# One PSUM pool of four banks for products and values, two banks lent as a third score slot, three scheduling rules, and longer assumed DMA latencies

## The chip, the cores and the metric

The kernel runs on one core of one Trainium2 chip. The metric is the device time of one execution in microseconds, the median of several runs. All runs in this document are of the state that the measurements call fast. Each kernel was timed in alternation with the kernel before on the same chip. A ratio below is the mean time of one kernel's fast runs over the mean time of the other's fast runs of the same rounds, so it is not quite the ratio of the medians that are quoted.

## The reference

Two blocks, each run twice in turn, on 2048 tokens of width 640, in bf16:

```python
x = A_x
x = x + _A_ref(_layernorm(x), ...)   # attention: 32 heads of 20, 4 segments of 512 tokens
x = x + _B_ref(_layernorm(x), ...)   # feed-forward: 640 -> 1728 -> relu -> 640
x = x + _A_ref(_layernorm(x), ...)
x = x + _B_ref(_layernorm(x), ...)
# inside _A_ref, for each segment s of 4:
    p = softmax(qs @ ks.T * scale + causal mask); a_dot = p @ vs
    a_mem = phi(qs) @ M / (phi(qs) @ z + 1e-6)           # memory of the earlier segments
    o = g * a_mem + (1 - g) * a_dot
    M += phi(ks).T @ vs;  z += sum(phi(ks))
```

## The kernel before: the parts that matter here

The kernel is written as about thirty generators ("streams"), one for each kind of work. A list scheduler inside the Python program takes the next operation of some stream again and again, with assumed durations, and writes out one fixed instruction list for each engine. At run time there is no choice any more. If an engine's next instruction has to wait, what stands behind it in the list is held up too: in one run below (a_latold) TensorE stood still for 2.18 us in front of one product. The assumed numbers therefore shape the order, and nothing else.

```python
X = Slot(ps[:, 0:2, :], "SX")                    # two score slots of two PSUM banks
Y = Slot(ps[:, 2:4, :], "SY")
OD = Slot(ps[:, 4, :], "OD")                     # one bank for p @ v ("values")
MISC = [Slot(ps[:, 5 + k, :], "misc%d" % k) for k in range(3)]   # three for all other products
...
def turn(slot_sem, dst, src, waits):             # a transpose by DMA
    ... yield dma("sp", ..., e.dma_start_transpose(dst, src), waits,
            issue=max(1400.0, 140.0 * n), lat=2000.0, rate=270.0, holds=True)
...
# scores(): a round is two halves (two heads each), half k goes to (X, Y)[k]
both = pe(221.0, fns, a[1] + b[1] + a[0].tks + b[0].tks, take=[a[0], b[0]], mode="rows")
...  # while no layer norm of block B has begun, one half alone is allowed too ("lone")
# exps(): ACT reads a whole slot (128x1024) and frees it
tx = yield act(1024, lambda e: e.activation(dst, src, ACT.Exp, scale=SCALE), sc + pw)
bkp.release(tx)
...
# apply(): p @ v of four heads
yield Acq([OD])
tk = yield pe(540.0, fns, mk + vt + OD.tks, mode="cols", lag=COLS_LAG)
...
yield from values_done(a, s, g, tk)              # at a segment's end: wait for "dm", then free v
```

Scores and values use a quarter of the array for each matmul, four at a time. So do 160 small ones of the feed-forward (128*32 in the trace). All other matmuls use the whole array. I call the q, k and v projections of segments 1 and 2 of the first attention *early products*: they need no attention result, so TensorE can do them while segment 0's attention goes on. *Filler* is any product that TensorE can do while attention waits for something. Of the tiles named below, o_sb holds the attention output and oT its transpose, xnT a transposed layer norm, and om_sb the part read from the memory. A *spill* is a transfer to DRAM.

The softmax here doesn't subtract the row's maximum and nothing guards it: scores larger than these inputs give would overflow.

## Time and profile before

| | kernel before |
|---|---|
| time | 582.72 us median of 4 runs (582.07 to 584.15) |
| profiled span | 580.5 us |
| TensorE busy | 562.3 us, 97% |
| ACT, VectorE busy | 413.4 us, 400.8 us |

Lines of the page of the kernel before: the span, the busy time of each engine with its share and instruction count, then busy tenths in 40 equal slices and the granted TensorE clock. In all views PE is TensorE and PEld its weight loads, ACT is ScalarE, DVE is VectorE, POOL is GpSimd; L1048 is line 1048 of that kernel.

```profile
span 580.5 us, 13203 instructions
...
PE 562.3 (97%) x5442; PEld 307.0 (53%) x5442; DVE 400.8 (69%) x1048; ACT 413.4 (71%) x528; POOL 185.7 (32%) x291
...
PE   7999989899999999999999999999999999999998
...
PEclk9999998999999999999999999999999999999999
```

TensorE is the bottleneck, but its busy time hides much. The Trainium skill says so ("Perfetto Trace Analysis", Identifying the Most-Contended Engine: matmul busy time is a bad metric for how close a kernel is to roofline, because matmuls are pipelined), and this trace agrees: a 128x320 matmul is recorded at 299 ns, and the next one starts 136 ns after it. I therefore worked from start times. A whole-array matmul of N columns lets the next one start N/2.4 + 2.6 ns later (136 ns for 320 and 216 ns for 512 columns, as the trace has them; the 21-column ones start 25 ns apart), and about 96 ns more when the tiling of the array changes. Time between two starts beyond that, where it is over 20 ns, I call **lost**. Lost time inside a record of the trace that gives the clock as 0.5 counts as lost to the clock, as far as half rate explains it; the rest counts as lost to waits. Every "lost" below is worked out in this way from one profile.

In the kernel before, 23.2 us are lost: 5.1 in 0 to 40 us, 2.7 in 40 to 80, 6.5 in 80 to 120, and 8.9 later. The stretches of the kernel before, with the busy time of each engine, the granted clock, the DMA share and GB/s:

```profile
core 0: us, PE busy (x) PEld busy (x) DVE busy (x) ACT busy (x) POOL busy (x), PEclk, DMA share, GB/s
30.00:62.00 32.00, 30.71 (x403) 17.36 (x406) 27.84 (x72) 28.18 (x37) 13.23 (x20) 1.00 0.81 192
62.00:80.00 18.00, 17.45 (x202) 9.07 (x195) 17.10 (x50) 16.18 (x22) 7.46 (x12) 1.00 0.79 186
80.00:120.00 40.00, 36.11 (x496) 20.11 (x495) 34.67 (x103) 34.80 (x43) 15.28 (x23) 0.96 0.76 175
120.00:200.00 80.00, 79.05 (x837) 41.27 (x835) 60.83 (x157) 64.36 (x76) 31.45 (x49) 1.00 0.37 86
200.00:320.00 120.00, 118.10 (x1128) 59.90 (x1127) 95.05 (x227) 100.25 (x121) 47.62 (x73) 1.00 0.54 109
320.00:480.00 160.00, 156.58 (x1460) 81.81 (x1458) 115.65 (x315) 119.48 (x152) 52.84 (x80) 1.00 0.39 82
```

From 80 to 120 us TensorE is even recorded as idle for 3.9 us, and the clock is 0.96. What it waits for there (engine and line, who ended the wait; us in total, times, longest):

```profile
PEld ps L1048 <- ACT PT L1100: 4.1, 8, 1.2
PEld ps L941 <- DVE om_sb L952: 2.8, 4, 1.1
...
PE ps L941 <- DVE om_sb L952: 1.4, 3, 0.8
```

L1048 is the scores: they wait for ACT's exps to free both slots. L941 is the reads of the memory. The 0.96 is one record of 3.4 us at clock 0.5, from 88.3 us on. The timeline shows it in the 128x320 matmuls, 0.47 us each where 0.30 is usual:

```profile
87.90 0.86 PE L590 MATMUL ps<-wo_r,oT 128*128 128x320 bf16 x4
88.56 0.47 PE L587 MATMUL ps<-wo_r,oT 128*128 128x320 bf16 x1
88.82 0.47 PE L590 MATMUL ps<-wo_r,oT 128*128 128x320 bf16 x1
```

The last view is ACT's timeline in the middle of segment 0. Two exps take 1.94 us, and then ACT does other work or waits for scores:

```profile
45.38 1.92 ACT L1100 ACTIVATE PT<-ps 128x1024 bf16<-128x1024 f32 x2
48.29 1.94 ACT L1100 ACTIVATE PT<-ps 128x1024 bf16<-128x1024 f32 x2 [0.98 <-PE ps L1048]
50.12 0.60 ACT L764 ACTIVATE w_r<-ps 128x512 bf16<-128x512 f32 x1
51.14 1.94 ACT L1100 ACTIVATE PT<-ps 128x1024 bf16<-128x1024 f32 x2 [0.42 <-PE ps L1048]
```

### The profile page before, as it was taken

The numbers are of one execution on the slowest core, as the hardware profiler recorded it, in microseconds if no ns is written. First come the engines' busy times: TensorE is split into PE (matmuls) and PEld (weight loads), VectorE is DVE, ScalarE is ACT, GpSimd is POOL, SyncE is SP. The second block draws the span as 40 slices with busy tenths as digits, with TensorE's granted clock in tenths as the row PEclk, the third lists the DMA queues.
The fourth block names the chain that finished last, engine by engine and source line by source line (L and its number), as shares of the span: only waits on it lengthen the run. The fifth ranks groups of instructions, "written<-read, shape, count | busy, mean of one in ns | idle before, by whom it ended". The sixth has DMA issues, their size and how long they took to land.

```text
span 580.5 us, 13203 instructions
## 1 busy us (share of the span) xinstructions
PE 562.3 (97%) x5442; PEld 307.0 (53%) x5442; DVE 400.8 (69%) x1048; ACT 413.4 (71%) x528; POOL 185.7 (32%) x291
## 2 busy tenths in 40 slices
PE   7999989899999999999999999999999999999998
PEld 6754545455544443555436545555454554665655
DVE  4879998956988778878678982789836784353202
ACT  5688998878788878887998786877767778214140
POOL 4234343433434334344333441144412443100000
PEclk9999998999999999999999999999999999999999
DMA  8578886633162622964278031781317611433101
GB/s 261 136 159 188 211 210 161 154 116 71 32 172 58 111 41 82 194 98 66 57 190 147 2 66 35 171 166 20 65 38 178 117 42 19 87 69 33 59 1 46
DMA packets 125741, 59.90 MB, mean 103 GB/s; under 512 B 104562, under 2 KB 115570, under 8 KB 125682
## 3 DMA queue, kind: packets, MB, share of 16 engines
q1 hardware_dynamic: 125552, 58.90, 45.9%
q8 instruction: 43, 0.70, 0.5%
q10 hardware_dynamic: 130, 0.16, 0.1%
q14 instruction: 16, 0.13, 0.1%
HBM read 20.57 MB, written 12.85 MB: 58 GB/s over the span
## 4 chain that ended last, share of the span: by engine, by line
PE 77%; DVE 14%; DMA 5%; ACT 2%; issue 0%; SPq 0%; POOL 0%
PE ps L590 50%; PE ps L587 11%; PE ps L1048 7%; PE ps L1133 4%; DVE stats L598 2%; DMA otk<-otu 2%; PE ps L1172 2%; ACT PT L1100 1%; PE ps L992 1%; PE ps L941 1%; DVE x_sb L1253 1%; DVE xn_tok L640 1%; DVE stg L763 1%; DVE o_sb L1225 1%; DVE otu L1143 1%; PE ps L1304 1%
## 5 line engine op out<-in xcount | busy, mean ns | idle before, releaser
L1100 ACT ACTIVATE PT<-ps 128x1024 bf16<-128x1024 f32 x320 | 310.0, 1022 | 74.5 <-PE ps L1048 74.1
L1112 POOL TENSOR_SCALAR_AFFINE_SELECT PT<-PT 128x512 bf16<-128x512 bf16 x256 | 164.3, 659 | 293.6 <-ACT PT L1100 293.6
L590 PE MATMUL ps<-w_r,hT 128*128 128x320 bf16 x768 | 124.5, 299 | 0.0
L590 PE MATMUL ps<-xnT,w_r 128*128 128x512 bf16 x416 | 114.1, 379 | 0.0
L1253 DVE TENSOR_TENSOR x_sb<-x_sb,ps 128x320 bf16<-128x320 bf16 x128 | 60.7, 481 | 69.2 <-PE ps L590 68.6
L590 PEld LDWEIGHTS ps<-w_r,hT 128*128 128x128 bf16 x768 | 72.9, 98 | 32.1 <-issue 5.4
L1048 PE MATMUL ps<-pad 20*128 20x512 bf16 (+3 forms) x1024 | 64.4, 302 | 2.4 <-ACT PT L1100 2.4
L590 PEld LDWEIGHTS ps<-xnT,w_r 128*128 128x128 bf16 x416 | 39.3, 98 | 43.4 <-issue 4.2
L598 DVE BATCH_NORM_STATS2 stats<-x_sb 128x6 f32<-128x320 bf16 x124 | 55.1, 474 | 3.6 <-DMA x_sb<-in_A_x_dram 3.0
L1331 ACT ACTIVATE hT<-ps 128x512 bf16<-128x512 f32 x60 | 36.0, 599 | 23.2 <-PE ps L590 23.0
L590 PE MATMUL ps<-wo_r,oT 128*128 128x320 bf16 x256 | 47.6, 305 | 0.0
L1048 PEld LDWEIGHTS ps<-pad 20*128 20x128 bf16 x1024 | 18.7, 92 | 51.7 <-ACT PT L1100 27.2
L587 PE MATMUL ps<-xnT,w_r 128*128 128x512 bf16 x104 | 39.6, 381 | 0.5 <-DVE M_sb L1004 0.5
L1329 DVE TENSOR_SCALAR hT<-ps 128x512 bf16<-128x512 f32 x44 | 30.1, 684 | 12.8 <-PE ps L590 12.5
L1143 DVE CAST otu<-ps 128x512 bf16<-128x512 f32 x43 | 29.4, 683 | 12.8 <-PE ps L1133 12.2
L590 PE MATMUL ps<-wv_r,xnT 128*128 128x320 bf16 x192 | 36.6, 300 | 0.0
L1133 PE MATMUL ps<-PT,v_aug 128*21 128x512 bf16 (+3 forms) x768 | 34.7, 301 | 0.0
L590 PE MATMUL ps<-xnT,wq_r 128*128 128x512 bf16 (+1 forms) x140 | 33.7, 349 | 0.0
L590 PE MATMUL ps<-xnT,wk_r 128*128 128x512 bf16 (+1 forms) x140 | 33.6, 349 | 0.0
L909 ACT ACTIVATE stg<-stg 128x512 bf16<-128x512 bf16 x50 | 31.1, 635 | 2.5 <-DVE rtmp L907 2.5
L612 POOL TENSOR_TENSOR rstd<-lnU,mhalf 128x4 f32<-128x4 f32 (+1 forms) x17 | 16.9, 997 | 45.4 <-DVE lnU L608 40.2
L590 PEld LDWEIGHTS ps<-wo_r,oT 128*128 128x128 bf16 x256 | 24.1, 99 | 12.0 <-issue 3.4
(114 smaller groups left out, 699.1 us busy)
## 6 DMA issues: line engine op xcount, KB each, us to landing
pad<-scr SPq DMA_DIRECT2D x124, 80.0 KB
scr<-stg SPq DMA_DIRECT2D x34, 256.0 KB, 3.0
out_dram<-x_sb SPq DMA_DIRECT2D x16, 160.0 KB, 1.8
w_r<-in_B_w_dram SPq DMA_DIRECT2D x10, 216.0 KB, 3.6
w_r<-in_B_w_dram SPq DMA_DIRECT2D x13, 160.0 KB, 2.8
x_sb<-in_A_x_dram SPq DMA_DIRECT2D x10, 160.0 KB, 3.3
scr<-w_r SPq DMA_DIRECT2D x5, 256.0 KB, 3.3
x_sb<-in_A_x_dram SPq DMA_DIRECT2D x3, 320.0 KB, 7.4
```

What stands on the lines that cost most here:

```text
L587: bk, tk = yield pe(mm_ns(n), [(lambda e, bk, a=a, b=b: e.matmul(bk.ap[:, 0:n] if len(b.shape) == 2 else bk.ap[:, 0:n].rearrange("p (i n) ...
L590: tk = yield pe(mm_ns(n), [(lambda e, k=k, a=a, b=b, bk=bk: e.matmul(bk.ap[:, 0:n] if len(b.shape) == 2 else bk.ap[:, 0:n].rearrange("p (i ...
L598: tk = yield dve(320, 1, lambda e, c2=c2: e.bn_stats(stats6[:, t % 12, c2, :], x_sb[:, t, c2 * 320:(c2 + 1) * 320]), xt)
L909: te = yield act(512, lambda e, q=q: e.activation(q, q, ACT.Exp), [tr] + p, psum=False)
L1048: fns.append([(lambda e, z=z, j=j, hh=hh, N=N, o=o, sl=sl: e.matmul(ps[:, hh, o:o + N], sl.ap[32 * hh:32 * hh + DH, z, 0, 128 * j:128 * j ...
L1100: tx = yield act(1024, lambda e, dst=dst, src=src: e.activation(dst, src, ACT.Exp, scale=SCALE), sc + pw)
L1112: tm = yield pool(600.0, lambda e, reg=reg: e.affine_select(out=reg, in_=reg, pattern=[[0, 4], [1, 128]], compare_op=ALU.is_ge, fill=0.0, ...
L1133: fns.append((lambda e, j=j, hh=hh: e.matmul(OD.ap[32 * hh:32 * hh + DH + 1, 128 * j:L], VAUG[vx(a, s)][:, j, 4 * g + hh, :], pt.ap[:, hh, ...
L1143: te = yield evac(L, 1, lambda e: e.tensor_copy(dst, OD.ap), lambda e: e.activation(dst, OD.ap, ACT.Copy), [tk] + OTU[0].tks)
L1253: ta = yield dve(320, 1, lambda e: e.tensor_tensor(x_sb[:, t, 320 * hf:320 * hf + 320], x_sb[:, t, 320 * hf:320 * hf + 320], bk.ap[:, 0:32 ...
L1329: th = yield evac(512, 1, lambda e, dc=dc, bk=bk: e.tensor_scalar(hT[:, dc, :], bk.ap[:, :], 0.0, None, ALU.max), lambda e, dc=dc, bk=bk: ...
L1331: lambda e, dc=dc, bk=bk: e.activation(hT[:, dc, :], bk.ap[:, :], ACT.Relu), [tk] + HT.tks)
```

## The change

The intent: products and values share four banks. While segment 0 is in progress, two of the four become a third score slot, so that scores of one round can be written while ACT still reads the round before. v is freed by a stream of its own, so that the values need not wait for the memory write. Ties between streams of equal priority go to the earlier segment. Scores are now always issued as whole rounds. The scheduler assumes longer latencies for transposes and for spills to DRAM. The cut below leaves out two small edits: first_heads now waits for the first two staging tiles in both of its passes, and the memset of the old values bank is gone.

```diff
-        OD = Slot(ps[:, 4, :], "OD")
-        MISC = [Slot(ps[:, 5 + k, :], "misc%d" % k) for k in range(3)]
+        Z = Slot(ps[:, 4:6, :], "SZ")
+        MISC = [Slot(ps[:, 4 + k, :], "misc%d" % k) for k in range(4)]
+        LENT = MISC[0:2]
+        SC = [X, Y]
 ...  # the order of operations with equal start times
-                key = (round(start + late), 0.5 if op.urgent else prio, n)
+                key = (round(start + late), 0.5 if op.urgent else prio, self.rank[id(st[1])], n)
 ...  # the fixed point before each choice
-                    if st[2] is not had and not isinstance(st[2], (Op, Either)):
-                        moved = moved or st[2] is None
+                    moved = moved or st[2] is not had
 ...  # turn(): lat=2000.0 -> 2400.0; spill(): lat 1500 (default) -> 2300.0
 ...  # scores()
+            LEND_FROM, LEND_TO = ("stg", 0, 0, 4, 1), ("sc", NSEG * 0 + G // 2 - 1, 4, 1)
+                    if LEND_FROM in S.events and LEND_TO not in S.events:
+                        for sl in LENT:
+                            if sl in MISC and sl.free:
+                                MISC.remove(sl)
+                                Z.tks = Z.tks + sl.tks
+                                if not any(x in MISC for x in LENT):
+                                    SC.append(Z)
+                    elif LEND_TO in S.events and Z in SC and Z.free:
+                        SC.remove(Z) ...  # and both banks back to MISC
+                    ready = sorted((s for s in SC if s.free), key=...)
+                    if len(ready) < 2 ...: return None, None        # never half a round
 ...  # apply()
-            yield Acq([OD])
-            tk = yield pe(540.0, fns, mk + vt + OD.tks, mode="cols", lag=COLS_LAG)
+            OD, tk = yield pe(540.0, fns, mk + vt, acq=MISC, mode="cols", lag=COLS_LAG)
-            yield from values_done(a, s, g, tk)
+            if g == G - 1:
+                S.set("valued", a, s, tks=[tk])
 ...
+        def free_v(a, s):
+            tk = yield Need("valued", a, s)
+            dmt = yield Need("dm", a, s)
+            VA[vx(a, s)].release(*tk, *dmt)
 ...  # each(): rank = NSEG * a + s of the segment in work;  S.add(1, each(free_v))
```

The 5442 matmuls are the same ones in both kernels; only their order and the banks differ.

More of the change, by code (lines that the diff above doesn't have):

```diff
@@ L174, in __init__ @@
         self.dma_free = 0.0
+        self.rank = {}
         self.mode = "full"
@@ L178, in add @@
         self.streams.append([prio, gen, None, None, False])
+        self.rank[id(gen)] = 0
     def at(self, tk):
@@ L618, in turn @@
             tk = yield dma("sp", slot_sem, 32768 * n, lambda e: e.dma_start_transpose(dst, src), waits,
-                           issue=max(1400.0, 140.0 * n), lat=2000.0, rate=270.0, holds=True)
+                           issue=max(1400.0, 140.0 * n), lat=2400.0, rate=270.0, holds=True)
             return tk
@@ L837, in spill @@
                     scr[s % 2, 128 * c:128 * c + 128, :], STGS[sx(a, s)][:, c].rearrange("p n t -> p (n t)")),
-                    ev + before, issue=350.0)
+                    ev + before, issue=350.0, lat=2300.0)
                 S.set("packed", a, s, c, tks=[tk] + direct)
@@ L847, in first_heads @@
                 ev = []
-                if z == 0:
-                    for n in range(2):
-                        t = yield Need("stg", 0, 0, 0, n)
-                        ev = ev + t
+                for n in range(2):
+                    t = yield Need("stg", 0, 0, 0, n)
+                    ev = ev + t
                 sem = sems[z]
@@ L1029, in scores, with half @@
             pads = {}
-            def half(h):
+            LEND_FROM, LEND_TO = ("stg", 0, 0, 4, 1), ("sc", NSEG * 0 + G // 2 - 1, 4, 1)
+            def half(h, slot):
                 m, u, k = HALVES[h]
@@ L1047, in half @@
                     N = L - 128 * j
-                    fns.append([(lambda e, z=z, j=j, hh=hh, N=N, o=o, sl=sl: e.matmul(
-                        ps[:, hh, o:o + N], sl.ap[32 * hh:32 * hh + DH, z, 0, 128 * j:128 * j + 128],
+                    fns.append([(lambda e, z=z, j=j, hh=hh, N=N, o=o, sl=sl, q=hh % 2: e.matmul(
+                        slot.ap[:, q, o:o + N], sl.ap[32 * hh:32 * hh + DH, z, 0, 128 * j:128 * j + 128],
                         sl.ap[32 * hh:32 * hh + DH, z, 1, 128 * j:L]),
                         y == len(parts) - 1 and hh % 2 == 1) for hh in (2 * k, 2 * k + 1)])
-                return (X, Y)[k], pd, fns
+                return slot, pd, fns
             h = 0
             while h < len(HALVES):
+                took = []
                 def ask(h=h):
-                    a = half(h)
-                    if a is None or not a[0].free:
+                    if LEND_FROM in S.events and LEND_TO not in S.events:
[6 more added lines that the diff above has]
+                    elif LEND_TO in S.events and Z in SC and Z.free:
+                        SC.remove(Z)
+                        for sl in LENT:
+                            sl.tks = Z.tks
+                            MISC.append(sl)
+                    ready = sorted((s for s in SC if s.free), key=lambda s: max([S.at(t) for t in s.tks], default=0.0))
+                    if len(ready) < 2 or h + 1 >= len(HALVES):
                         return None, None
-                    lone = pe(221.0, [f for fs in a[2] for f in fs], a[1] + a[0].tks, take=[a[0]], mode="rows")
-                    b = half(h + 1) if h + 1 < len(HALVES) else None
-                    if b is None or not b[0].free:
-                        return None, lone
+                    a, b = half(h, ready[0]), half(h + 1, ready[1])
+                    if a is None or b is None:
+                        return None, None
+                    took[:] = ready[:2]
                     fns = []
@@ L1067, in ask @@
                             fns += z[2][y] if y < len(z[2]) else []
-                    both = pe(221.0, fns, a[1] + b[1] + a[0].tks + b[0].tks, take=[a[0], b[0]], mode="rows")
-                    ready = [max([S.at(t) for t in z[1] + z[0].tks], default=0.0) for z in (a, b)]
-                    return both, (lone if ("hx", 0, 0) not in S.events and max(ready[0], S.free["pe"]) + LONE_NS < max(ready[1], S.free["pe"]) else None)
+                    return pe(221.0, fns, a[1] + b[1] + a[0].tks + b[0].tks, take=[a[0], b[0]], mode="rows"), None
                 tks = yield Either(ask)
-                tks = tks if isinstance(tks, list) else [tks]
-                if len(tks) == 2 and len(ROUNDS[HALVES[h][1]]) > len(ROUNDS[HALVES[h + 1][1]]):
-                    tks = tks[::-1]
-                for tk in tks:
+                for tk, sl in zip(tks, list(took)):
                     m, u, k = HALVES[h]
-                    S.set("sc", m, u, k, tks=[tk])
+                    S.set("sc", m, u, k, tks=[sl, tk])
                     if (u, k) == (4, 1):
@@ L1090, in exps @@
                     ex = []
-                    for k, bkp in enumerate((X, Y)):
+                    for k in range(2):
                         sc = yield Need("sc", m, u, k)
+                        bkp, sc = sc[0], sc[1:]
                         if u == 2:
@@ L1132, in apply @@
                 for hh in range(4):
-                    fns.append((lambda e, j=j, hh=hh: e.matmul(
+                    fns.append((lambda e, OD, j=j, hh=hh: e.matmul(
                         OD.ap[32 * hh:32 * hh + DH + 1, 128 * j:L], VAUG[vx(a, s)][:, j, 4 * g + hh, :],
@@ L1148, in apply @@
                 S.set("otu", n // 2, tks=EVAC[n // 2])
-            yield from values_done(a, s, g, tk)
-        def values_done(a, s, g, tk):
             if g == G - 1:
-                dmt = yield Need("dm", a, s)
-                VA[vx(a, s)].release(tk, *dmt)
-                if (a, s) == (0, 0):
-                    S.set("v00", tks=VA[2].tks)
+                S.set("valued", a, s, tks=[tk])
[3 more added lines that the diff above has]
+            VA[vx(a, s)].release(*tk, *dmt)
+            if (a, s) == (0, 0):
+                S.set("v00", tks=VA[2].tks)
         EVAC = {}
@@ L1163, in apply_by_token @@
                 yield Acq(OSB)
-            yield Acq([OD])
-            od = OD.ap[:, 0:336].rearrange("p (i hh e) -> p i hh e", i=NJ, hh=4)
-            tk = None
+            od4 = lambda bk: bk.ap[:, 0:336].rearrange("p (i hh e) -> p i hh e", i=NJ, hh=4)
+            tk = OD = None
             for i in range(NJ):
@@ L1171, in apply_by_token @@
                         for j in range(i + 1):
-                            fns.append((lambda e, i=i, hh=hh, j=j: e.matmul(
-                                od[:, i, hh, :], pt.ap[:, hh, PT_OFF[j] + 128 * (i - j):PT_OFF[j] + 128 * (i - j) + 128],
+                            fns.append((lambda e, b=None, OD=OD, i=i, hh=hh, j=j: e.matmul(
+                                od4(b or OD)[:, i, hh, :], pt.ap[:, hh, PT_OFF[j] + 128 * (i - j):PT_OFF[j] + 128 * (i - j) + 128],
                                 VAUG[vx(a, s)][:, j, 4 * g + hh, :], start=(j == 0), stop=(j == i)),
                                 i == NJ - 1 and hh == 3 and j == i))
-                    tk = yield pe(25.2 * len(fns), fns, (waits + OD.tks) if i == 0 and h2 == 0 else [])
+                    if i == 0 and h2 == 0:
+                        OD, tk = yield pe(25.2 * len(fns), fns, waits, acq=MISC)
+                    else:
+                        tk = yield pe(25.2 * len(fns), fns)
             pt.release(tk)
+            od = od4(OD)
             rd = yield Acq(RDEN)
@@ L1189, in apply_by_token @@
             S.set("o", n, tks=[to])
-            if n + 1 == BY_TOKEN:
-                z = yield dve(512, 1, lambda e: e.memset(OD.ap, 0.0), [to])
-                OD.tks = [z]
-            yield from values_done(a, s, g, tk)
+            if g == G - 1:
+                S.set("valued", a, s, tks=[tk])
         def turn_pair(m):
@@ L1360, in each, with g @@
         def each(f):
-            for a, s in AS:
-                yield from f(a, s)
+            def g():
+                for a, s in AS:
+                    S.rank[id(me)] = NSEG * a + s
+                    yield from f(a, s)
+            me = g()
+            return me
         def items(f, count):
@@ L1371, in bass_interleave_layers__memory_aug_infini_attn__dense_activation_relu__prompt_kernel @@
         S.add(1, items(apply, 2 * NSEG * G))
+        S.add(1, each(free_v))
         S.add(1, items(turn_pair, NSEG * G))
```

## The prediction

> **What bounds it now.** TensorE's issue order. The first part of the page shows PE busy 562.3 of 580.5 us, but busy time flatters: the Trainium skill ("Perfetto Trace Analysis", Identifying the Most-Contended Engine) calls it a bad metric because matmuls are pipelined, and this trace agrees: a 128x320 matmul is recorded at 299 ns but the next one starts 136 ns later (512 columns: 379 and 216 ns). So I worked from matmul start times in the timeline. Entering or leaving the packed score or value matmuls costs about 96 ns more (512 columns then scores: 312 against 216). Priced so, all matmuls need about 551 us; starts later than that add about 23 us of stalls: 5.1 in 0-40 us (start-up), 2.7 in 40-80, 6.5 in 80-120, about 9 afterwards, almost none in the last 110 us (feed-forward alone). Of the 6.5, about 1.7 are one 3.4 us record at clock 0.5 (88.3-91.7 us), just after a group of stalls; the rest are scores waiting for exps of both slots, and memory reads waiting for om_sb. Only these stalls can be won.
>
> **What the change does to the order** (built program, PE):
> - Mode switches 392 -> 385: about -0.7 us. Two rounds issued half by half become whole.
> - With the third score slot, rounds 7 to 20 stand 1.1-1.8 us of PE work apart instead of 2.7. Segment 0's scores end after 53 us of PE work, not 67. A round's two exps step 2 x 0.905 = 1.81 us on ACT, so ACT now paces this stage: summed over rounds the PE work is short by 2.3 us, before latencies. Products there have two banks instead of three plus OD, and all their evacuations are on DVE (0.60 us step for 512 columns), mixed with norms. I expect 3-5 us of new stalls at about 33-62 us.
> - Output projection and feed-forward of segment 0 begin 7-9 us of PE work earlier, and the thin rounds of before (1.0-1.8 us of PE work, around 72-92) are gone: after the lending nearly all rounds stand 2.3-2.9 us apart, which covers two exps plus one other ACT operation. I expect the 80-120 stalls to fall from 6.5 to about 2, the low-clock record among them.
> - One pool of four banks afterwards, with values no longer on one bank, v freed outside the values' stream, and larger assumed latencies for transposes and spills: about 9 us of later stalls become about 6.
>
> **Sum.** -0.7 (switches), +4 less 1-2 already there (lending), -4.5 (80-120), -3 (later): about -5 us. From 583.2: **578.5 us**; 8 in 10 between 573.5 and 584.0. Chances: faster by over 2% 0.04 (needs half of all stalls to go, and 5 us of start-up stay), within 2% 0.94, slower by over 2% 0.02.
>
> **What the profile would show.** Right: between about 33 and 60 us ACT busy near 95% with exps back to back at 0.9 us steps, PE waiting for exps (scores after ACT) or for DVE evacuations; PE busy under that of before there, and higher in 80-120; no clock record of 0.5 at 80-120; segment 0's fifth rounds done some 10 us earlier; the last 100 us the same. Wrong: PE as busy as before at 33-60 (then the gain is larger), or stalls of 80-120 unchanged or only moved to later.
>
> **What would make it wrong.** PE so thin in the lending stage that the clock falls to half for one or more 3.4 us records (1.7 us each). In-order evacuations on DVE behind norms holding both product banks: each late one stops PE. Memory reads still use one bank of the pool each time, so their stalls may stay.

## More of the kernel before

The chips differ a little: the median of the kernel before was between 582.7 and 584.7 us. Runs are therefore compared by their ratios.

## The result, and the profile after

The changed kernel took 572.81 us (median of 4 runs, 572.75 to 573.2) beside 582.72 us: ratio 0.9828 (95% interval 0.9807 to 0.9849). Run again it took 573.34 us beside 583.29, ratio 0.983 (0.9817 to 0.9844). That is 9.9 us faster, twice the 5 us that I had forecast, and just below the low end of my range, 573.5.

Of the page of the changed kernel:

```profile
span 571.0 us, 13253 instructions
...
PE 558.2 (98%) x5442; PEld 306.3 (54%) x5442; DVE 406.4 (71%) x1056; ACT 408.3 (72%) x519; POOL 186.3 (33%) x291
...
PE   7999999999999999999999999999999999999998
...
PEclk9999999999999999999999999999999999999999
```

The same stretches, from the second profile of the changed kernel (span 571.6 us):

```profile
30.00:62.00 32.00, 30.17 (x443) 16.55 (x444) 26.88 (x72) 30.95 (x36) 16.43 (x26) 1.00 0.80 190
62.00:80.00 18.00, 16.85 (x226) 9.35 (x225) 16.46 (x43) 16.78 (x24) 7.81 (x12) 1.00 1.01 209
80.00:120.00 40.00, 39.95 (x524) 21.42 (x522) 38.18 (x112) 36.35 (x48) 16.35 (x25) 1.00 0.64 151
120.00:200.00 80.00, 78.68 (x804) 42.58 (x804) 67.32 (x175) 64.73 (x76) 31.12 (x48) 1.00 0.50 108
200.00:320.00 120.00, 119.48 (x1111) 61.09 (x1110) 91.39 (x222) 93.19 (x113) 44.62 (x67) 1.00 0.47 101
320.00:480.00 160.00, 158.59 (x1475) 81.81 (x1474) 119.22 (x313) 124.05 (x155) 54.99 (x83) 1.00 0.40 82
```

TensorE is a little less busy up to 80 us, and from 80 to 120 us it has no gap. ACT is busy for 30.95 of the 32 us up to 62 us. Its timeline there (first profile) is one unbroken run of exps:

```profile
44.25 11.41 ACT L1113 ACTIVATE PT<-ps 128x1024 bf16<-128x1024 f32 x12
55.81 1.02 ACT L1113 ACTIVATE PT<-ps 128x1024 bf16<-128x1024 f32 x1 [0.16 <-PE ps L1051]
```

Twelve exps took 11.41 us, 0.95 us each, where the kernel before needed about 2.8 us for each two. From 80 to 120 us what is left of the waits is short (longest 0.5 us, where it was 1.2). The sum for the scores' weight loads fell only from 4.1 to 3.3 us, but matmuls were recorded as busy for 39.95 of these 40 us all the same, so these waits of the weight loads were nearly all covered by running matmuls. The reads of the memory are no longer among the largest:

```profile
PEld ps L1051 <- ACT PT L1113: 3.3, 8, 0.5
PEld ps L593 <- issue: 1.5, 7, 0.2
```

Lost time, in us, in the windows that the prediction used:

| | 0-40 | 40-80 | 80-120 | later | sum |
|---|---|---|---|---|---|
| before | 5.1 | 2.7 | 6.5 | 8.9 | 23.2 |
| after | 5.5 | 4.5 | 0.5 | 4.7 | 15.2 |
| difference | +0.4 | +1.8 | -6.0 | -4.2 | -8.0 |

With 7 fewer changes of tiling (392 to 385, 96 ns each, 0.7 us) this is 8.7 of the 9.5 us by which the span fell. The remaining 0.8 us I have not traced; gaps under the 20 ns cut are not counted.

### The profile page after: what moved, and what is told of

It is laid out like the page before. It is cut to its first block, busy times and chain, and to the rows that moved or that the text cites. A ratio compares the mean times of both kernels' runs of the same rounds, so it can differ in the third digit from the quotient of the medians.

```text
span 571.0 us, 13253 instructions
## 1 busy us (share of the span) xinstructions
PE 558.2 (98%) x5442; PEld 306.3 (54%) x5442; DVE 406.4 (71%) x1056; ACT 408.3 (72%) x519; POOL 186.3 (33%) x291
## 4 chain that ended last, share of the span: by engine, by line
PE 82%; DVE 9%; DMA 3%; ACT 3%; SPq 1%; issue 0%; POOL 0%
PE ps L593 53%; PE ps L590 11%; PE ps L1051 8%; PE ps L1145 5%; PE ps L1184 2%; ACT PT L1113 2%; DVE stats L601 2%; PE ps L943 1%; PE ps L994 1%; DVE xn_tok L643 1%; DMA beta_bc<-in_A_beta_dram 1%; DVE x_sb L1267 1%; PE ps L1318 1%; DMA hT<-xn_tok 1%; DMA oT<-o_sb 1%; DVE o_sb L1239 1%
## 5 line engine op out<-in xcount | busy, mean ns | idle before, releaser
L593 PE MATMUL ps<-w_r,hT 128*128 128x320 bf16 x768 | 121.8, 299 | 0.0
L1345 ACT ACTIVATE hT<-ps 128x512 bf16<-128x512 f32 x55 | 32.9, 599 | 33.7 <-PE ps L593 33.6
L1343 DVE TENSOR_SCALAR hT<-ps 128x512 bf16<-128x512 f32 x49 | 33.2, 681 | 14.2 <-PE ps L593 14.2
L766 DVE CAST stg<-ps 128x512 bf16<-128x512 f32 (+1 forms) x45 | 28.4, 630 | 20.2 <-PE ps L593 20.1
L1155 DVE CAST otu<-ps 128x512 bf16<-128x512 f32 x39 | 26.7, 684 | 12.3 <-PE ps L1145 12.0
L593 PE MATMUL ps<-xnT,wk_r 128*128 128x512 bf16 (+1 forms) x140 | 35.1, 349 | 0.0
L593 PE MATMUL ps<-xnT,wq_r 128*128 128x512 bf16 (+1 forms) x140 | 33.8, 349 | 0.0
L643 DVE TENSOR_SCALAR xn_tok<-x_sb,mv,rstd 128x640 bf16<-128x640 bf16 x60 | 30.1, 536 | 2.7 <-POOL rstd L615 2.7
```

What stands on the lines that cost most here:

```text
L593: tk = yield pe(mm_ns(n), [(lambda e, k=k, a=a, b=b, bk=bk: e.matmul(bk.ap[:, 0:n] if len(b.shape) == 2 else bk.ap[:, 0:n].rearrange("p (i ...
L643: nm = lambda e, bx, t, k: e.tensor_scalar(bx.ap[:, k * D:k * D + D], x_sb[:, t + k, :], mv[:, t + k, 0:1], rstd[:, t + k:t + k + 1], ALU. ...
L1343: th = yield evac(512, 1, lambda e, dc=dc, bk=bk: e.tensor_scalar(hT[:, dc, :], bk.ap[:, :], 0.0, None, ALU.max), lambda e, dc=dc, bk=bk: ...
L1345: lambda e, dc=dc, bk=bk: e.activation(hT[:, dc, :], bk.ap[:, :], ACT.Relu), [tk] + HT.tks)
```

## The experiments

The theory for the large part is about **the stretch without filler**. In the trace of the kernel before, the last early product starts at 83.1 us and the first feed-forward product of segment 0 at 110.8 us. For 27.7 us TensorE has, besides attention, only the 40 products of segment 0's output projection and the 25 of segment 3's k projection (about 7 and 6 us from start to start), and two score slots pace attention by a loop from scores to exps and back. In the changed kernel segment 0's scores are done at 63.0 us instead of 76.1, the early products still last until 98.8 us, and the first feed-forward product starts at 100.3: a stretch of 1.5 us. The ends of the stretch on TensorE's timeline, of the kernel before and then of the changed kernel (of four early products merged in a line, the last starts about 0.65 us after the first):

```profile
82.46 1.03 PE L590 MATMUL ps<-hT,wq_r 128*128 128x512 bf16 x4
110.83 0.38 PE L587 MATMUL ps<-xnT,w_r 128*128 128x512 bf16 x1
```

```profile
98.16 1.03 PE L593 MATMUL ps<-hT,wq_r 128*128 128x512 bf16 x4
100.27 0.38 PE L590 MATMUL ps<-xnT,w_r 128*128 128x512 bf16 x1
```

The theory is that the third slot moves attention forward, into a time in which filler abounds.

The rivals were these: the shared pool or the small scheduling rules carry the gain; or the order of the kernel before was an unlucky draw, since any edit here reshuffles thousands of instructions. Two parts of the change were never undone alone: the rule of whole rounds, and the waits in first_heads.

All 18 runs were correct. "Scores" is when segment 0's scores were done, "stretch" as above, both in us. The lost columns are waits; time lost to the clock is in the last column, with the number of records at clock 0.5 between 20 and 500 us.

| run | median us | ratio to before | scores | stretch | lost 30-62 | 62-120 | 120 on | clock |
|---|---|---|---|---|---|---|---|---|
| before | 582.72 | 1 | 76.1 | 27.7 | 1.8 | 6.0 | 8.9 | 1.6 (1) |
| b_m85 | 592.44 | 1.0144 | 76.9 | 34.5 | 2.4 | 7.7 | 11.7 | 6.3 (3) |
| b_lat | 586.22 | 1.0025 | 75.1 | 33.0 | 0.3 | 4.8 | 12.2 | 5.4 (2) |
| a_odown_nolend | 579.56 | 0.9927 | 73.6 | 29.9 | 0.1 | 7.8 | 5.6 | 2.0 (1) |
| a_nolend | 584.35 | 1.0000 | 76.3 | 32.3 | 0.8 | 7.2 | 7.7 | 5.7 (3) |
| a_lend1 | 574.97 | 0.9856 | 71.4 | 23.6 | 1.6 | 3.5 | 6.0 | 1.6 (1) |
| a_lend2 | 575.20 | 0.9873 | 66.9 | 11.5 | 2.2 | 3.2 | 5.1 | 1.5 (1) |
| changed, first | 572.81 | 0.9828 | 63.0 | 1.5 | 2.9 | 2.2 | 4.6 | 0 |
| after_again | 573.34 | 0.9830 | 62.9 | 1.5 | 3.0 | 2.1 | 5.3 | 0 |
| a_lend7 | 579.48 | 0.9943 | 64.1 | 0.2 | 2.9 | 6.1 | 6.3 | 3.3 (1) |
| a_odown | 581.90 | 0.9953 | 62.9 | 12.1 | 4.4 | 5.6 | 7.5 | 1.6 (1) |
| a_m75 | 573.89 | 0.9847 | 63.2 | 1.3 | 3.3 | 2.1 | 5.1 | 0 |
| a_m70 | 578.27 | 0.9891 | 62.6 | 4.0 | 2.9 | 3.0 | 7.2 | 1.6 (1) |
| a_norank | 577.59 | 0.9888 | 63.0 | 2.9 | 3.1 | 3.0 | 8.3 | 0 |
| a_nofreev | 577.51 | 0.9888 | 63.2 | 1.7 | 3.4 | 2.6 | 6.0 | 2.4 (1) |
| a_spillold | 575.81 | 0.9846 | 64.4 | 4.1 | 4.1 | 3.2 | 6.6 | 0 |
| a_turnold | 580.97 | 0.9933 | 64.1 | 3.8 | 4.4 | 3.9 | 9.1 | 0 |
| a_latold | 584.32 | 1.0001 | 65.4 | 2.6 | 3.1 | 3.8 | 10.1 | 4.5 (2) |
| a_t32_m75 | 571.81 | 0.9777 | 64.3 | 2.3 | 3.9 | 2.3 | 2.0 | 1.6 (1) |
| t32_again | 571.03 | 0.9792 | 63.3 | 2.3 | 3.8 | 1.5 | 2.0 | 0 |

a_lend7 has a second record of half clock, at 10 us; its 1.6 us is in the 3.3, but not in the count. Its profile is also of the slowest of its four executions (581.4 us; the others took 578.7 to 579.6), so its losses are at the high end. Figures of one profile can differ by 0.1 from the table above.

### Lending, the pool, both undone; and a reshuffled kernel before

**a_nolend**: lending off.

```diff
-                    if LEND_FROM in S.events and LEND_TO not in S.events:
+                    if False:
```

> The changed kernel with the lending switched off: two score slots throughout, values and products share four banks. Theory (the early stage: lending moves segment 0's scores 14 us of TensorE work forward, which costs about 2 us of stalls before 80 us and saves about 6 us between 80 and 120 us, a half-clock record of 1.7 us among them): time 576 to 578 us, stalls of 4 us or more back between 70 and 120 us, about 4 us of stalls after 120 us as in the changed kernel. Rival (the shared pool and the rest of the change carry the gain, lending nothing): 574 us or less, and few stalls at 80-120 us without any third slot.

Measured: 584.35 us, ratio 1.000 (0.9966 to 1.0033). The whole gain is gone, more than either theory had. Of the 12.1 us by which its span is longer than the changed kernel's, about 9 are lost at 62 to 120 us (5.0 to waits, 4.1 to the clock) and 4.7 after 120 us (3.1 and 1.6), while 2.1 are saved at 30 to 62 us. Nothing is lent after 120 us, so that the 4.7 us come from lending is not shown: the order there changed too. Of 40 us from 80 to 120 TensorE is busy for 33.8, and the clock is 0.83:

```profile
80.00:120.00 40.00, 33.81 (x475) 19.01 (x473) 33.82 (x105) 33.24 (x42) 16.50 (x24) 0.83 0.73 156
```

**a_odown**: values on a bank of their own (with the memset of that bank which the kernel before also had), products on three, two of them lent.

```diff
-        MISC = [Slot(ps[:, 4 + k, :], "misc%d" % k) for k in range(4)]
+        MISC = [Slot(ps[:, 4 + k, :], "misc%d" % k) for k in range(3)]
+        ODS = [Slot(ps[:, 7, :], "OD")]
-            OD, tk = yield pe(..., acq=MISC, ...)      # and the same in apply_by_token
+            OD, tk = yield pe(..., acq=ODS, ...)
```

> The changed kernel with values on a bank of their own again (products three banks, of which two are lent in segment 0, so one is left). Theory: in the lending stage every product group waits for the evacuation of the one bank, stalls before 80 us rise from 10 to over 16 us; after 120 us the stalls go back from 4.4 towards the 9 us of the kernel before; 582 us or more. Rival (the shared pool does nothing, only lending counts): within 1.5 us of the changed kernel's 572.8.

Measured: 581.90 us, ratio 0.9953 (0.9916 to 0.999). The scores are as early as in the changed kernel (62.9 us), but 4.4 instead of 2.9 us are lost at 30 to 62 us, the stretch is 12.1 us, and 5.6 us of waits and a half-clock record return after it. The waits before 80 us (10.8 us with the start-up) stayed under the 16 that I had expected; the total came out as expected.

**a_odown_nolend**: both edits together.

> The changed kernel with neither lending nor shared pool: what is left is v's own stream, ties by segment, scores always in whole pairs, and the larger assumed latencies. Theory (lending and pool are the gain): 580 to 583 us, as the kernel before less 0.7 us for 8 fewer mode switches. Rival (the small scheduling rules are the gain): 576 us or less.

Measured: 579.56 us, ratio 0.9927 (0.9888 to 0.9966), a little below the theory's range and above the rival's. It is *faster* than a_nolend. So the shared pool gains nothing by itself in these orders: without lending it goes with 0.7% more time, and with lending with 1.3% less. What it does is leave two product banks during lending instead of one.

**b_m85**: the kernel before, one assumed margin changed.

```diff
-PE_MARGIN = 80.0
+PE_MARGIN = 85.0
```

> The kernel before with one scheduling margin for TensorE set to 85 instead of 80 ns, which only reshuffles the order (PE mode switches 392 to 387). Theory: within 2 us of the kernel before (581 to 584.5), with stalls at 80-120 us of 4 us or more again, since two score slots remain. Rival (the order before was an unlucky draw, with a half-clock record by accident): 578 us or less, and no half-clock record.

Measured: 592.44 us, ratio 1.0144 (1.0108 to 1.0179). The expectation missed by 8 us, to the slow side. The order of the kernel before was not an unusually bad one; a neighbour of it is 1.4% worse. All five two-slot kernels have a stretch of 28 to 35 us, and waits of 4.8 to 7.8 us at 62 to 120 us, with half-clock records besides. These records are no accident of the profiled execution: the granted clock over a whole execution (one record of 3.4 us makes 0.997) was 0.983 to 0.994 in every execution of b_m85, b_lat, a_nolend and a_odown_nolend, and 1.0 in all nine of the changed kernel.

### The dose: how long is the third slot kept

```diff
-  LEND_TO = ("sc", NSEG * 0 + G // 2 - 1, 4, 1)      # pair 3, the end of segment 0
+  LEND_TO = ("sc", 1, 4, 1)                          # a_lend1; a_lend2: 2; a_lend7: 7
```

> The changed kernel with the third score slot withdrawn after item pair 1 of segment 0 instead of after pair 3 (about 4 fast score rounds instead of 14). Theory (what counts is the stretch between the last early product of segments 1 and 2 and the first feed-forward product, when TensorE has little but attention to do: 27.7 us in the kernel before, 1.5 us in the changed one, 32.3 us without lending; fewer fast rounds leave more of it): segment 0's scores done at 72 us, a stretch of 18 to 26 us, losses at 62-120 us of 5 to 10 us, time 577 to 582 us. Rival (an order that happens to be good, not the number of fast rounds): no relation, 573 us or as bad as without lending.

> The third slot withdrawn after item pair 2 (about 9 fast rounds). Theory: segment 0's scores done at 67 to 68 us, stretch without products 8 to 15 us, losses at 62-120 us of 3 to 6 us, time 574 to 578 us, between the changed kernel and the run with pair 1. Rival: out of line with the others.

> The third slot kept until the end of segment 1 (pair 7). Theory: segment 0 as in the changed kernel (scores done at 63 us); after that two product banks for 40 us more cost waits of 2 to 4 us, and nothing is left to win at 80-120 us, so 573 to 577 us. Rival (more score slots are better as such): below 572 us.

Measured: a_lend1 574.97 us (0.9856, 0.9826 to 0.9885), a_lend2 575.20 us (0.9873, 0.9844 to 0.9902), a_lend7 579.48 us (0.9943, 0.9915 to 0.9972). The times at which the scores are done (76.3, 71.4, 66.9, 63.0 us for no, 4, 9 and 14 fast rounds) and the stretches (32.3, 23.6, 11.5, 1.5 us) follow the dose as the theory had them. The time does not follow it evenly: the first four fast rounds bring 1.4 of the 1.7%, and a_lend1 beat its expected range, with a stretch that is still 23.6 us long. The intervals of a_lend1 and a_lend2 reach into that of the changed kernel, so what the later rounds add is not clear of noise. Keeping the slot through segment 1 costs 1.2%, and a_lend7 came out 2.5 us over its range: TensorE waits 6.1 us at 62 to 120 us, with two product banks. Keeping it longer still could not be tried: the build with pair 11 has a race on the weights of the second feed-forward matrix.

### Is it the order alone

**a_m75** and **a_m70**: the changed kernel with PE_MARGIN at 75 and 70.

> The changed kernel with the scheduling margin for TensorE at 75 instead of 80 ns, which only reshuffles the order. Theory: stretch without products below 5 us again, losses at 62-120 us of 1.5 to 4 us, no half-clock record, 572 to 576 us; the spread against the changed kernel is what order alone is worth, above all after 120 us. Rival (luck of the order): 578 us or more.

> The changed kernel with the TensorE margin at 70 ns, the order with the evenest score rounds of those built (one round after segment 0 under 2.3 us of TensorE work, against 7). Theory: losses at 62-120 us of 1.5 to 3.5 us, losses after 120 us of 3 to 4.5 us, no half-clock record, 569 to 573 us. Rival (the changed kernel is already at what this structure gives): 573 to 576 us.

Measured: a_m75 573.89 us (0.9847, 0.9823 to 0.987), as expected. a_m70 578.27 us (0.9891, 0.9854 to 0.9927), 5 us over its range, although its score rounds were expected to be the evenest: 3.6 us of its waits end with an o_sb transpose landing. So a reshuffle alone is worth up to 0.6% here, and nearly all of it falls after 120 us. The gain at 62 to 120 us stands in both. Over all runs, the eight kernels with the shared pool, the new latencies (or longer ones) and a slot lent within segment 0 only lie at 0.9777 to 0.9891 of the kernel before, with waits of 1.5 to 3.5 us at 62 to 120 us; the five two-slot kernels lie at 0.9927 to 1.0144, with 4.8 to 7.8 us. The two groups, put together afterwards, do not overlap, which an unlucky order of the kernel before would not explain. But lending alone is not enough: a_odown, a_lend7, a_turnold and a_latold have it too, and lie at 0.9933 to 1.0001.

### The small rules

**a_norank**, **a_nofreev**: ties by segment, or v's own stream, undone.

```diff
-                    S.rank[id(me)] = NSEG * a + s                     # a_norank
-        S.add(1, each(free_v))                                        # a_nofreev
+                yield from free_v(a, s)    # in the values' stream, at a segment's end
```

> The changed kernel without ties by segment. Theory (the advance of segment 0 is the gain, the tie rule is worth no more than a reshuffled order): 572 to 576.5 us, stretch without products below 6 us, losses after 120 us of 4 to 8 us. Rival (the tie rule is what made the losses after 120 us fall from 9.0 to 4.7): those losses back at 8 us or more, 577 us or more.

> The changed kernel with v freed inside the values' stream again. Theory: as above, 571.5 to 576 us, losses after 120 us of 4 to 8 us. Rival (freeing v apart is what made the losses after 120 us fall): 8 us or more of them, 577 us or more.

Measured: 577.59 us (0.9888, 0.9857 to 0.9919) and 577.51 us (0.9888, 0.9864 to 0.9913), both 0.6% worse than the changed kernel. Both meet the numbers that I had set for the rival (over 577 us; 8.3 us lost after 120 us, and 6.0 with 2.4 to the clock). But a_m70, where no rule was undone, has the same loss (7.2 with 1.6 to the clock, 578.27 us). The threshold that I had set lies within the order's own spread, so these two runs do not tell what the rules are worth.

**a_latold**: the old assumed latencies. **a_turnold**, **a_spillold**: one of the two.

```diff
-  lat=2400.0, rate=270.0, holds=True)          # turn(); a_latold, a_turnold
+  lat=2000.0, rate=270.0, holds=True)
-  ev + before, issue=350.0, lat=2300.0)        # spill(); a_latold, a_spillold
+  ev + before, issue=350.0)
```

> The changed kernel with the scheduler's old assumed latencies of transposes and spills. Theory: 572.5 to 577 us; waits for transposed tiles (phk, oT, xnT) at least 0.5 us more than in the changed kernel, since consumers are put too close behind. Rival (the assumed latencies are what made the losses after 120 us fall): 8 us or more of them, 577 us or more.

> The changed kernel with the assumed latency of transposes alone back at 2000 ns (spills at the new 2300). Theory (TensorE's order is fixed when the kernel is built; the o_sb transposes landed 3.5 to 5.8 us after issue in the three traces looked at, 3.5 being what 2000 ns assumes, so products placed right behind them stop TensorE): TensorE waits for oT and xnT of 2 to 6 us against 0.6 in the changed kernel, 576 to 585 us. Rival (the run with both old latencies was an unlucky order, latencies do nothing by themselves): waits for oT and xnT under 1.5 us and 572 to 576 us.

> The changed kernel with the assumed latency of spills alone back at 1500 ns. Theory (spills feed pads and phi, which are asked for long before use): no wait for scr or pad on TensorE over 0.5 us; 572 to 577 us, order noise. Rival (spills are the cause): 580 us or more.

Measured: a_latold 584.32 us (1.0001, 0.9976 to 1.0027), far over the theory's range and within the rival's (577 us or more, with 8 us or more lost after 120 us; it was 10.1): the whole gain is gone although the scores are early and the stretch is short. a_turnold 580.97 us (0.9933, 0.9908 to 0.9957), a_spillold 575.81 us (0.9846, 0.982 to 0.9871), as expected. Of the two numbers, that of the transposes goes with the larger loss. In a_latold the output projection stands too close behind the transpose of o_sb. Its waits (us in total, times, longest):

```profile
PEld ps L590 <- DMA oT<-o_sb: 7.0, 5, 2.3
...
PE ps L590 <- DMA oT<-o_sb: 5.5, 5, 2.2
```

and its worst case on the timeline, where TensorE stood still for 2.18 us and then worked at half clock (0.45 us for 320 columns):

```profile
76.11 1.16 PE L1184 MATMUL ps<-v_aug,PT 128*128 128x21 bf16 x40
79.45 0.45 PE L590 MATMUL ps<-wo_r,oT 128*128 128x320 bf16 x1 [2.18 <-DMA oT<-o_sb]
79.69 1.27 PE L593 MATMUL ps<-wo_r,oT 128*128 128x320 bf16 x4
```

The o_sb transposes of that trace landed 3.5 to 5.6 us after their issue, with a median of 3.9. Waits for oT and xnT take 7.3 us of the lost time there, 0.6 and 1.3 in the two profiles of the changed kernel, and only 0.9 in the kernel before, which has the same old numbers. The old assumption comes to 3.5 us (2000 + 300 + 327680/270 ns), the new one to 3.9: the old one is the best case of that trace. In a_turnold, however, only 1.4 us of the waits end with oT or xnT, less than the 2 to 6 that I had expected. The rest is spread over om_sb (3.5 us), w_r (3.1) and others. That its order is worse is measured; that the latency itself makes it so is not shown.

**b_lat**: the new latencies in the kernel before. Without the change's fix to the fixed point the scheduler gets stuck there and nothing is built. The fix alone leaves the order of the kernel before exactly as it was (the built instruction lists are equal).

```diff
-                    if st[2] is not had and not isinstance(st[2], (Op, Either)):
-                        moved = moved or st[2] is None
+                    moved = moved or st[2] is not had
-  turn(): lat=2000.0;  spill(): lat 1500 (default)
+  turn(): lat=2400.0;  spill(): lat=2300.0
```

> The kernel before with the new latencies (and the fix without which the scheduler gets stuck, which alone leaves the order of before as it was). Theory (two score slots leave the stretch without products, whatever the latencies): 580 to 588 us, losses at 62-120 us of 7 us or more, stretch of 25 us or more, waits for transposes 1 us or less. Rival (latencies are the gain, in either kernel): 577 us or less.

Measured: 586.22 us, ratio 1.0025 (0.9986 to 1.0065), stretch 33.0 us, two half-clock records. The latencies alone bring nothing where the stretch stands, as the theory had it; its waits for transposes were 1.7 us, a little over the 1 us expected. In these runs, one order of each, lending came to nothing without the latencies, and the latencies to nothing without lending.

### More slack: a version that beats both

**a_t32_m75**: transposes assumed at 3200 ns, spills at 2700, PE_MARGIN 75. It was picked, for its slack, among the best of 56 such combinations by the scheduler's own estimate. That estimate is no measurement: the one that it liked best was a_m70.

```diff
-PE_MARGIN = 80.0
+PE_MARGIN = 75.0
-  turn(): lat=2400.0;  spill(): lat=2300.0
+  turn(): lat=3200.0;  spill(): lat=2700.0
```

> The changed kernel with transposes assumed at 3200 ns, spills at 2700, margin 75: a candidate. Theory: no wait for oT or xnT on TensorE over 0.3 us in sum, no half-clock record, 569.5 to 573 us. Rival (order noise decides): 573 to 578 us.

Measured: 571.81 us, ratio 0.9777 (0.9751 to 0.9802). TensorE's waits for oT and xnT are 0.06 us in sum, the waits after 120 us 2.0 us. One half-clock record, which I had not expected, fell at 50.2 us.

Both kernels were then run side by side on one chip, five rounds:

> The changed kernel itself, again, on the chip of the next run: both theories: ratio to the kernel before 0.980 to 0.985, no half-clock record between 20 and 500 us, waits of TensorE after 120 us of 4 to 5.5 us. If it comes out at 0.988 or worse, the first reading was a lucky state, and the undone parts lose less than they seem to.

> The candidate with transposes assumed at 3200 ns, side by side with the changed kernel on one chip. Theory (more slack behind transposes takes the rest of the waits for oT and xnT, about 0.6 us, and the order is a little better after 120 us, but one half-clock record costs 1.6 us): 0.995 to 0.999 of the changed kernel's time. Rival (no better): 1.000 or more.

Measured: the changed kernel 573.34 us, ratio 0.983 again; the candidate 571.03 us, ratio 0.9792 (0.9779 to 0.9805). By the ratios, which share the kernel before, the candidate takes 0.996 of the changed kernel's time; the intervals do not meet. Its stretches after 120 us:

```profile
120.00:200.00 80.00, 79.83 (x807) 42.38 (x805) 61.58 (x160) 62.13 (x75) 29.21 (x45) 1.00 0.39 85
200.00:320.00 120.00, 119.89 (x1155) 62.47 (x1153) 96.76 (x233) 100.39 (x121) 49.34 (x74) 1.00 0.53 109
320.00:480.00 160.00, 159.59 (x1485) 82.18 (x1484) 118.63 (x315) 125.61 (x156) 56.71 (x84) 1.00 0.40 83
```

In this profile no half-clock record was there; in the earlier profile of the same candidate (a_t32_m75) there was one. So a record can come and go with the same instruction list. Of the four executions of a_t32_m75, the two at a granted clock of 0.997 took 572.4 and 572.5 us and the two at 1.0 took 571.1 and 571.3: there a record went with about 1.3 us, less than the 1.6 that the counting gives.

## Why the prediction was wrong

The bottleneck, the place of the gain and its sign were right; the size was half of what was measured. The step that failed is the term for the stalls at 80 to 120 us: I let them fall from 6.5 to about 2 us, and they fell to 0.5. The later stalls were mis-sized in the same direction. And the sum was added up short: the terms as predicted make -5.2 to -6.2 us, while 583.2 to 578.5 is -4.7.

| step, as predicted | predicted us | measured us |
|---|---|---|
| mode switches 392 -> 385 | -0.7 | -0.7 (7 x 96 ns, by count) |
| lending stage: +4 less 1 to 2 already there | +2 to +3 | +1.8 (2.7 -> 4.5, at 40-80 us) |
| stalls at 80-120 us, 6.5 to about 2 | -4.5 | -6.0 (6.5 -> 0.5) |
| stalls later, about 9 to about 6 | -3 | -4.2 (8.9 -> 4.7) |
| start-up, unchanged | 0 | +0.4 |
| sum | about -5 | -8.7, and the span -9.5 |

- **"The 80-120 stalls fall from 6.5 to about 2"** was the step with the largest error in size, 1.5 us. I had counted how far apart the score rounds stand in TensorE work, and left 2 us for what the counting does not see. I had not asked what fills the time between rounds. The runs show that with the third slot the stretch between the last early product and the first feed-forward product closes to 1.5 us, and that the waits fall with it (2.1 to 2.2 us at 62 to 120 us in a_m75 and in both profiles of the changed kernel; 4.8 to 7.8 us in the five two-slot kernels). That the length of the stretch is what sets the waits is not shown: a_lend1 still has 23.6 us of it and loses 3.5 us there, while a_lend7 with 0.2 us and a_odown with 12.1 us lose 6.1 and 5.6.
- **"Later stalls, 9 to 6, by one pool of four banks"** was too small by 1.2 us, and its reason does not stand, so that it came this near is luck. a_nolend has the pool and 7.7 us of waits after 120 us, with 1.6 to the clock at 453 us besides; a_odown_nolend has no pool and 5.6 us. The later waits move between 2.0 and 12.2 us over the runs. The assumed latency of transposes is one cause that shows in waits (a_latold, and a_t32_m75 on the other side). For the rest, which part of the change made them 4.7 stays open: undoing a rule reshuffles the order, and a reshuffle alone is worth up to 0.6%.
- **"No clock record of 0.5 at 80-120"** was right; by the counting it was worth 1.6 us, where I had predicted 1.7. What I did not see is how much such records weigh on the other side: without lending they cost 5.7 us, and that is part of why undoing one piece gives the whole gain back.
- **The lending stage** came out as described: ACT busy 30.95 of 32 us, exps 0.95 us apart, TensorE waiting for exps and for VectorE's evacuations. It was 0.2 to 1.2 us cheaper than predicted. The fear of half clock there did not come true in the changed kernel; it did in one profile of a_t32_m75 (50.2 us).
- **Latencies** stood in the prediction only in a half-sentence, among the later stalls. With the old ones the changed kernel is no faster than the kernel before (a_latold), a loss as large as that of the lending. It is beyond the 0.6% of a reshuffle here, but not far beyond the 1.4% between the kernel before and b_m85, and each is one order.

## What to carry to other kernels

Find out when the bottleneck engine has filler and when it does not, and move the dependent chain forward into the time with filler; here two PSUM banks, lent for about 30 us, went with most of the gain at 62 to 120 us, and lending them for longer lost part of the gain again. Where the instruction order is fixed when the kernel is built, try assumed DMA latencies above the best case of the trace: with 3.5 us assumed for the transposes of o_sb, TensorE waited 1.4 and 7.3 us for oT and xnT (a_turnold, a_latold), with 3.9 us 0.6 and 1.3 us (two profiles of the changed kernel) but 3.6 us in a_m70, and with 4.7 us 0.06 us or less. These are single orders, so how much the slack itself gives is not shown. And before a small part of a change is given credit in such a kernel, reshuffle the order without it: two neighbours that differed in one margin alone were 0.6% apart, and two of the kernel before were 1.4% apart.

## What the Trainium skill lacked or had wrong

- "TensorE: Matmul & The Clock Gate", Part 1 (The HAM clock gate), says that the clock falls to half after at least one idle window of about 3.4 us. Far less went before it here. In the 20 profiles, cut into windows of 3.413 us from the trace's own clock records (15 to 500 us, windows that were not themselves at half clock), the clock fell after none of the more than 2700 windows with under 1.0 us lost to waits, after 10 of the 50 with 1.0 to 1.8 us, and after 9 of the 10 with 1.8 us or more. This is a count of what came together, not a test of the cause. The section on PSUM-queue depth-cycling tells of oscillation after micro-idles, without such a number. The length of the window agrees: the records are 3.4 or 6.8 us long.
- The same page (Back-to-back issue gap) gives about 131 ns per matmul as the sustained pace for 512 columns in a stream of weight loads and matmuls. Here such streams run at 216 ns (median of 804 whole-array starts in the kernel before, lowest 215), which is what the page calls the isolated formula.
- "TensorEngine Tiling (Array Packing)", Key Properties, says that changing the tiling mode drains TensorE, without a cost. Here it cost about 96 ns (medians 88 to 101 by kind of change): 312 against 216 ns after 512 columns, 392 times in the kernel before, so an estimated 38 us of its 580.
- "DMA: Bandwidth & Descriptors" has a bandwidth for a transpose by DMA but no time from issue to landing of one from SBUF to SBUF. Here the 128x1280 transposes of o_sb landed between 3.5 and 6.4 us after issue (16 in each of the 20 profiles, medians 3.55 to 4.07 us).
